# RWKV-5 followed by a squared-ReLU expert: one column of w_in read ahead, diagonal sums of twelve units by VectorE, and a new order table

## The chip, the cores and the metric

The kernel runs on one core of a Trainium2 chip. A core has five engines with a queue each: TensorE (matmuls; PE in the profile, PEld for its weight loads), VectorE (DVE), ScalarE (ACT), GpSimd (POOL) and SyncE (SP, which here only issues DMAs). All DMAs go through 16 DMA engines. On-chip data lies in SBUF, matmul results in eight PSUM banks. The metric is the device time of one execution in microseconds (us), lower is better.

## The reference

```python
def _attn_ref(r, k, v, w, u):            # B, H, S, D = 4, 8, 768, 48
    state = np.zeros((B, H, D, D))
    for t in range(S):
        cur = np.einsum('bhd,bhe->bhde', u[None] * kt, vt)
        y[:, :, t] = np.einsum('bhd,bhde->bhe', rt, state + cur)
        state = w[None, :, :, None] * state + np.einsum('bhd,bhe->bhde', kt, vt)
...
def _moe_ref(x, w_in, w_out):            # 3072 tokens, 384 -> 2048 -> 384
    h = x @ w_in
    r = np.maximum(h, 0.0)
    return (r * r) @ w_out
```

The output y of the recurrence, with the heads side by side, is x. Everything is float32 at the borders.

## The kernel before

The sequence is cut into six chunks of 128 steps. A chunk of one batch is a unit: unit i is batch i % 4 of chunk i // 4, 24 in all. Within a unit the recurrence is matrix work. r is multiplied by rising and k by falling powers of w (`scale`, VectorE, into `rkw`); both are transposed to `rkT`, by TensorE for units 0 to 5 (`turn`, `kb`, evicted by ScalarE) and by a transposing DMA for pairs of units from 6 on (`rkD`, SyncE). `at` makes the 128 x 128 products of k and r for each head, `mask` (VectorE) keeps the strict triangle as `am`, `y` multiplies by v and adds what comes from the running state `stb`. The state is updated by `s` (TensorE), `sadd` and `sdec` (VectorE) and `stb` (ScalarE).

The term with u concerns only the diagonal, where a step meets itself: for each head the sum over d of r k u, times v. Before, it goes like this: `rk` (line 353) multiplies the two halves of `rkT` on VectorE, for a pair at once from unit 6 on; TensorE sums over d with the small matrix `uwb` (u times w, placed head by head), four matmuls to a unit, in a step of its own for units 0 to 3 (line 389) and at the head of `s` for the others (line 410); `dv` (line 420, VectorE) multiplies by v, and `yb` (line 456) adds the result to y. `uwb` holds u times w because the powers in r and k leave one factor of w to be made good there.

The expert follows unit by unit. x is transposed (`xturn` and `xT`, or the DMA `xD`), `m1` multiplies by w_in (line 493), `relu` and `sqA` run on ScalarE, `sqD` is the same square on VectorE (line 510), `m2` multiplies by w_out (line 517), `osb` evicts and `out` stores. w_in comes in four quarters (`I`, line 288) and w_out in four (`O`, line 291), both on GpSimd's queue, where the v loads of units 0 to 5 (`vt`, line 311) stand too. The loads of r and k go over SyncE (lines 281 and 278).

The order of everything on every engine is written out by hand: the table `ORDER` is a list of steps, `name.unit.part@bank`, and a loop at the end of the kernel issues them one after the other. `fill.n` issues n matmuls on a constant tile, whose result nobody reads. What stands ahead of the table in the code (memsets, constants, the first DMAs) comes first on each queue.

Of the kernel before, what the change touches and what calls it, by code (L numbers as in the profile page):

```python
# [21 lines left out]
m1.0.0@7 kbT.1 mask.1.0 turn.2.1@2 relu.0.0 dv.1 rt.5.0 fill.2 y.1@1 rkT.2.1 m1.0.3@4 yb.1 end rt.5.1 s.1@5
scale.3.0 relu.0.3 wend xturn.1@7 rk.2 at.2@26 xT.1 kb.2@0 mask.2.1 sqA.0.0 kt.5.0 d.2@4 turn.3.0@3 vt.3 s.0@7
sadd.1 rkT.3.0 m1.0.2@1 kt.5.1 scale.3.1 kbT.2 O.0 m1.1.0@6 mask.2.0 vb.2 relu.0.2 vt.4 turn.3.1@3 dv.2 m1.1.3@5
rt.6 rkT.3.1 sadd.0 O.1 y.2@1 relu.1.0 kt.6 m1.1.2@0 yb.2 relu.1.3 vt.5 at.3@72 rk.3 relu.1.2 kb.3@4 mask.3.1
xturn.2@6 sqA.1.0 O.2 m1.0.1@5 scale.4.0 xT.2 s.2@0 O.3 sqD.0.3 d.3@2 relu.0.1 m1.1.1@1 vb.3 mask.3.0 turn.4.0@3
kbT.3 m1.2.0@6 scale.4.1 relu.1.1 dv.3 m1.2.1@4 rkT.4.0 sqD.1.3 sqA.0.2 y.3@7 m1.2.2@1 scale.5.0 relu.2.1 sqD.1.1
m1.2.3@2 relu.2.2 sqD.0.1 s.3@5 sqA.1.2 turn.4.1@4 m2.0.0@3 sadd.3 relu.2.3 sadd.2 m2.1.0@1 rkT.4.1 yb.3 relu.2.0
m2.1.1 rk.4 vb.4 scale.5.1 kb.4@7 stb.1 xturn.3@6 at.4@42 kbT.4 m2.0.1 mask.4.1 xT.3 stb.0 s.4@5 mask.4.0 turn.5.0@6
m1.3.0@2 sqD.2.1 rkT.5.0 y.4@0 dv.4 relu.3.0 turn.5.1@6 rt.8 sadd.4 m1.3.3@7 rkT.5.1 yb.4 m2.1.2 sqA.3.0 sqA.2.0  # L30
m2.0.2 kt.8 xturn.4@2 m2.0.3 xT.4 scale.6.0 kb.5@5 osb.0 m2.1.3 scale.7.0 relu.3.3 m1.3.1@2 vtS.6 kbT.5 vb.5
m1.4.0@6 scale.6.1 scale.7.1 at.5@75 relu.4.0 m2.2.0@0 mask.5.0 osb.1 rkD.6 sqA.4.0 m1.4.1@4 sqD.2.3 sqA.2.2 sqD.3.3
m1.4.2@1 relu.3.1 mask.5.1 m2.2.1 stb.3 sdec.4 m1.4.3@6 relu.4.2 rt.10 rk.5 y.5@5 sqA.4.2 scale.8.0 s.5@2 scale.8.1
relu.4.1 m2.2.2 scale.9.0 relu.4.3 vtS.8 m1.3.2@1 sqD.3.1 stb.4 m2.3.0@4 dv.5 relu.3.2 yb.5 m2.2.3 scale.9.1 kt.10
m2.3.1 osb.2 sadd.5 sqA.4.1 m2.4.0@1 sqD.4.3 vb.6 xturn.5@0 sdec.5 at.6@2376 xT.5 rk.6 rkD.8 m2.4.1 stb.2 mask.7.0
stb.5 m1.5.0@0 sqA.3.2 mask.6.0 s.7@7 relu.5.0 mask.7.1 m1.5.3@5 mask.6.1 s.6@2 relu.5.3 m2.4.2 dv.6 out.0 vb.8
y.6@3 dv.7 rt.12 y.7@0 yb.6 m1.5.1@6 yb.7 m2.3.2 sadd.6 relu.5.1 xD.6 scale.10.0 m2.4.3 sqA.5.0 scale.10.1 sqA.5.1
m2.3.3 sadd.7 vtS.10 osb.4 m1.5.2@6 scale.11.1 scale.11.0 m2.5.0@3 relu.5.2 sqD.5.3 kt.12 m2.5.1 sqA.5.2 rk.8
# [24 lines left out]
relu.14.5 sqD.14.3 m1.14.4@7 sqA.14.5 mask.18.0 vtS.22 m2.14.0@3 relu.14.4 dv.18 out.9 m2.15.1 mask.19.1 sqA.14.4
s.19@7 sqA.14.6 rk.20 m2.14.1 sdec.17 y.19@1 dv.19 stb.17 y.18@2 m2.14.2 yb.18 m1.16.0@6 yb.19 sadd.19 xD.18
m1.16.4@2 relu.16.0 sdec.16 m2.14.3 sadd.18 relu.16.4 out.11 m1.16.1@1 osb.14 vb.20 at.20@7256 m1.16.3@4 sqA.16.4
mask.20.1 stb.16 m1.16.2@3 rk.22 relu.16.3 m2.15.2 mask.21.1 relu.16.1 relu.16.2 s.20@4 m2.15.3 dv.20 sqA.16.1
m1.16.5@1 mask.20.0 sqA.16.2 sdec.18 m1.16.7@2 sqA.16.0 mask.21.0 relu.16.5 s.21@7 m1.18.7@6 sdec.19 relu.16.7
s.22@3 sqD.16.3 m1.18.3@1 sqA.16.5 osb.15 m1.18.1@2 vb.22 y.20@4 relu.18.1 m1.16.6@0 yb.20 relu.18.3 y.21@5 dv.21
relu.16.6 m1.18.4@4 sqD.16.7 stb.18 m2.17.0@1 yb.21 relu.18.4 dv.22 m2.16.0@0 xD.20 relu.18.7 sqA.18.1 m2.17.1
sqA.16.6 at.22@3567 out.12 out.15 m1.18.6@4 mask.22.0 out.14 m1.18.2@2 mask.22.1 relu.18.6 m2.17.2 mask.23.0  # L70
relu.18.2 mask.23.1 m2.16.1 stb.19 sqD.18.7 y.22@4 m2.16.2 s.23@2 m1.18.5@7 dv.23 m1.18.0@5 sqD.18.3 yb.22 m2.16.3
relu.18.0 m1.20.0@3 sqA.18.4 relu.18.5 m1.20.3@5 osb.16 m1.20.6@2 relu.20.3 out.16 y.23@6 sqA.18.0 sqD.20.3 m2.17.3
sqA.18.5 yb.23 m1.20.7@4 sqA.18.6 xD.22 sqA.18.2 m1.20.1@7 relu.20.7 m1.20.5@5 relu.20.0 sqD.20.7 m2.18.0@0
relu.20.6 m2.18.1 relu.20.5 sqA.20.6 m2.18.2 sqA.20.0 m2.19.0@5 m2.19.1 m1.20.2@4 m1.20.4@3 relu.20.2 m1.22.6@6
sqA.20.2 m1.22.3@4 relu.20.1 relu.20.4 m2.19.2 osb.17 m2.18.3 sqA.20.5 relu.22.6 m1.22.1@3 relu.22.3 m1.22.0@2
sqA.20.1 sqD.22.3 m2.19.3 relu.22.0 m1.22.7@1 osb.19 sqA.22.0 m2.21.0@2 sqA.20.4 m2.21.1 relu.22.1 m1.22.2@7
sqA.22.6 m1.22.4@6 relu.22.2 m1.22.5@5 relu.22.7 relu.22.4 m2.20.0@3 sqD.22.7 sqA.22.1 m2.21.2 osb.18 sqA.22.2
m2.20.1 relu.22.5 m2.22.0@7 sqA.22.5 m2.22.1 sqA.22.4 m2.20.2 m2.21.3 m2.20.3 osb.21 m2.22.2 out.21 osb.20 out.18
# [5 lines left out]
def kernel(  # L84
# [21 lines left out]
    NH = 6  # L106
# [516 lines left out]
```

## Time and profile before

| | |
|---|---|
| median of 3 runs | 170.97 us (170.62 to 171.13) |
| the profiled execution | 171.94 us |
| its span, first to last instruction | 170.2 us |
| TensorE matmul busy | 163.9 us, 96% |
| ScalarE busy | 129.8 us, 76% |
| VectorE busy | 122.3 us, 72% |
| GpSimd busy | 15.7 us, 9% |
| mean granted TensorE clock | 0.988 |

The profile is of one execution, taken by the hardware. Times in it are counted from the first instruction. Durations of instructions on one engine overlap a little at their ends, so the step from one start to the next is shorter than the duration when an engine runs without a gap. A row of a timeline has the start, the time to the end of the last of the group, the engine, the line and the operation, and in brackets the idle time ahead of it with what ended it.

### The profile page before, as it was taken

The numbers are of one execution on the slowest core, as the hardware profiler recorded it, in microseconds if no ns is written. First come the engines' busy times: TensorE is split into PE (matmuls) and PEld (weight loads), VectorE is DVE, ScalarE is ACT, GpSimd is POOL, SyncE is SP. The second block draws the span as 40 slices with busy tenths as digits, with TensorE's granted clock in tenths as the row PEclk, the third lists the DMA queues.
The fourth block names the chain that finished last, engine by engine and source line by source line (L and its number), as shares of the span: only waits on it lengthen the run. The fifth ranks groups of instructions, "written<-read, shape, count | busy, mean of one in ns | idle before, by whom it ended". The sixth has DMA issues, their size and how long they took to land.

```text
span 170.2 us, 4733 instructions
## 1 busy us (share of the span) xinstructions
PE 163.9 (96%) x1947; PEld 134.1 (79%) x1947; DVE 122.3 (72%) x243; ACT 129.8 (76%) x255; POOL 15.7 (9%) x36
## 2 busy tenths in 40 slices
PE   7959999999999999999999999999999999999993
PEld 7649999778787697886977887787889789688672
DVE  6567999876999989988988888989697662101100
ACT  3735999888796489698499679688699739599921
POOL 7770670000000000000000000000000000000000
PEclk9996999999999999999999999999999999999999
DMA  3999999999999899999999997998990501100044
GB/s 92 172 279 240 272 194 254 213 201 227 185 181 218 153 214 190 181 212 191 236 182 202 174 251 173 188 288 197 180 232 4 179 6 54 42 0 4 0 164 162
DMA packets 91493, 28.86 MB, mean 170 GB/s; under 512 B 82864, under 2 KB 90672, under 8 KB 91472
## 3 DMA queue, kind: packets, MB, share of 16 engines
q1 hardware_dynamic: 88416, 23.99, 67.5%
q0 software_dynamic: 2624, 4.33, 12.9%
q8 instruction: 15, 0.25, 0.6%
q10 hardware_dynamic: 432, 0.25, 0.6%
q14 instruction: 6, 0.05, 0.1%
HBM read 20.50 MB, written 4.72 MB: 148 GB/s over the span
## 4 chain that ended last, share of the span: by engine, by line
PE 87%; DMA 6%; DVE 3%; SPq 2%; issue 1%; DVEq 0%
PE bank L493 36%; PE bank L517 34%; DMA rt<-in_r_dram 4%; PE bank L369 4%; PE bank L441 3%; DMA xT<-yb 2%; PE bank L398 2%; PE bank L447 2%; SPq L281 2%; PE bank L533 2%; PE bank L333 1%; PE bank L410 1%; PE bank L345 1%; PE bank L216 1%; PE bank L477 1%
## 5 line engine op out<-in xcount | busy, mean ns | idle before, releaser
L493 PE MATMUL bank<-xT,w_in_q 128*128 128x256 bf16 (+1 forms) x720 | 72.6, 251 | 0.1
L501 ACT ACTIVATE gr<-bank 128x512 f32<-128x512 f32 x96 | 55.3, 604 | 19.0 <-PE bank L493 15.2
L517 PE MATMUL bank<-w_out_q,g 128*128 128x384 bf16 x368 | 68.6, 326 | 0.0
L493 PEld LDWEIGHTS <-w_in_q 128*128 128x128 bf16 x720 | 63.8, 113 | 3.9 <-DMA xT<-yb 0.3
L517 PEld LDWEIGHTS <-g 128*128 128x128 bf16 x368 | 34.3, 98 | 18.1 <-issue 0.2
L508 ACT ACTIVATE g<-gr 128x512 bf16<-128x512 f32 x68 | 41.2, 636 | 0.2
L377 DVE TENSOR_TENSOR am<-bank,smask 128x512 bf16<-128x512 f32 x48 | 31.3, 684 | 7.4 <-PE bank L369 6.6
L510 DVE TENSOR_TENSOR g<-gr 128x512 bf16<-128x512 f32 x28 | 19.0, 686 | 17.2 <-ACT gr L501 17.2
L524 ACT COPY osb<-bank 128x384 f32<-128x384 f32 x23 | 11.0, 480 | 5.7 <-PE bank L517 5.6
L456 DVE TENSOR_TENSOR yb<-bank,dv 128x384 bf16<-128x384 f32 x24 | 12.9, 553 | 3.2 <-PE bank L447 2.3
L420 DVE TENSOR_TENSOR dv<-vb,bank 128x384 f32<-128x384 bf16 x24 | 13.0, 548 | 2.2 <-PE bank L410 1.4
L432 ACT CAST stb<-st 128x384 bf16<-128x384 f32 x20 | 10.2, 522 | 0.6 <-DVE st L428 0.6
L301 DVE TENSOR_TENSOR rkw<-rt,wpos 128x384 bf16<-128x384 f32 x18 | 9.8, 551 | 0.8 <-DMA rt<-in_r_dram 0.7
L301 DVE TENSOR_TENSOR rkw<-kt,wneg 128x384 bf16<-128x384 f32 x18 | 9.7, 551 | 0.8 <-DMA kt<-in_k_dram 0.8
L337 ACT COPY rkT<-bank 128x512 bf16<-128x512 bf16 x12 | 7.0, 590 | 3.4 <-PE bank L333 3.4
L216 PE MATMUL bank<-warm 128*128 128x128 bf16 x87 | 8.4, 265 | 1.1 <-DVE warm L161 1.1
L441 PE MATMUL bank<-vb,am 128*128 128x48 bf16 x192 | 8.9, 185 | 0.0
L428 DVE TENSOR_TENSOR st<-st,wend 128x384 f32<-128x384 f32 x16 | 8.8, 550 | 0.0
L424 DVE TENSOR_TENSOR st<-bank,st 128x384 f32<-128x384 f32 x16 | 8.7, 549 | 0.0
L441 PEld LDWEIGHTS <-am 128*128 128x128 bf16 x192 | 7.9, 97 | 0.8
L369 PE MATMUL bank<-rkT 64*128 64x128 bf16 x192 | 8.2, 221 | 0.2 <-ACT rkT L337 0.2
L216 PEld LDWEIGHTS <-warm 128*128 128x128 bf16 x87 | 7.0, 121 | 1.2 <-DVE warm L161 1.0
(75 smaller groups left out, 120.8 us busy)
## 6 DMA issues: line engine op xcount, KB each, us to landing
out_dram<-osb SPq DMA_DIRECT2D x23, 192.0 KB, 2.4
rt<-in_r_dram SPq DMA_DIRECT2D x9, 384.0 KB, 5.8
kt<-in_k_dram SPq DMA_DIRECT2D x9, 384.0 KB, 5.2
vt<-in_v_dram SPq DMA_DIRECT2D x9, 384.0 KB, 4.5
w_in_q<-in_moe_w_in_dram POOLq DMA_DIRECT2D x4, 384.0 KB, 8.3
w_out_q<-in_moe_w_out_dram POOLq DMA_DIRECT2D x4, 384.0 KB, 8.8
vt<-in_v_dram POOLq DMA_DIRECT2D x6, 192.0 KB, 7.3
kt<-in_k_dram SPq DMA_DIRECT2D x11, 96.0 KB, 5.2
```

The lines of the kernel that those rows point to most:

```text
L216: nc.tensor.matmul(out=banks[0][:, :128], lhsT=warm, rhs=warm, start=True, stop=True)
L301: nc.vector.tensor_tensor(t["rkw"][:, x, :, :, :D], pair(src), pair(wneg if x else wpos), ALU.mult)
L369: nc.tensor.matmul(out=t["at"][o][:, p, :], lhsT=t["rkT"][sl, 1, p, :], rhs=t["rkT"][sl, 0, p, :], start=True, stop=True,)
L377: nc.vector.tensor_tensor(am, t["at"][o], smask.unsqueeze(1).to_broadcast([C, HP, C]), ALU.mult)
L420: nc.vector.tensor_tensor(t["dv"], t["vb"], t["d"].unsqueeze(2).to_broadcast([C, H, D]), ALU.mult)
L441: nc.tensor.matmul(out=y[:, 2 * p + o, :], lhsT=t[f"am{o}"][:, p, :], rhs=t["vb"][:, 2 * p + o, :], start=(o == 0 and p == 0), stop=c == 0 ...
L456: nc.vector.tensor_tensor(t["yb"], t["y"], t["dv"].rearrange("p h d -> p (h d)"), ALU.add)
L493: nc.tensor.matmul(out=t["h", s][:, a], lhsT=turned, rhs=chunks[c]["xT"][:, b : b + m, n, :], start=(n == 0), stop=(n == NK - 1),)
L501: nc.scalar.activation(t["gr", s], t["h", s], AF.Relu)
L508: nc.scalar.activation(g, x, AF.Square)
L510: nc.vector.tensor_tensor(g, x, x, ALU.mult)
L517: nc.tensor.matmul(out=t["o"], lhsT=chunks[units[i][0]]["g"][:, f, units[i][1], :], rhs=w_out_q[f // 4][:, f % 4, :], start=(f == 0), stop ...
```

## The change

Three things change, and a new table places them.

`ahead` is a tile of 128 x 1 that nobody reads. A DMA on GpSimd's queue fills it with the first column of the first 128 rows of w_in, ahead of the memsets and DMAs for `wu`, which become a step `wu` at the head of the table. The logarithm `lnw` becomes a step too.

For units 12 to 23 the diagonal sum leaves TensorE. `dx` multiplies r and k as they lie in `rkw`, without the transpose, for a pair; `du` multiplies by `uw`, a row of u times w on every partition; `dr` adds up the 48 elements of each head into `dd`. All three are on VectorE. `dv` then takes `dd`. The `rk` products and the four matmuls of each of these units go, and the last chunk's `s` steps with them, which held nothing else. The row `uw` is made once on GpSimd from two broadcast loads, `uB` and `wB`, and lies in the place of `lnat`. `dv` has two buffers for pairs and not four for units. `rk`'s buffers serve `dx`.

Four squares (`sqD.12.3`, `sqD.14.3`, `sqD.16.3`, `sqD.18.3`) become `sqA`. There are 76 fill matmuls, before 87. The parameters `stbP` and `outP` that the diff brings are in no row of the table.

```diff
 ORDER = """
-kt.0.0 kt.0.1 rt.0.0 rt.1.0 I.0 rt.1.1 vt.0 ktA.1.0 lnat.0 fill.26 log@4567 kt.1.1 lnat.1 ids rt.2.0 w.1 upper w.0
...
+wu rt.0.0 kt.0.0 kt.0.1 rt.1.0 lnw rt.1.1 vt.0 ktA.1.0 lnat.0 fill.26 log@4567 kt.1.1 lnat.1 w.0 ids rt.2.0 w.1
...
+    ahead = const.tile([128, 1], F32)
+    nc.gpsimd.dma_start(out=ahead, in_=moe_w_in[:128, :1])
     wu = const.tile([HP, 2, 2, 64], F32)
-    nc.gpsimd.memset(wu[:, 0], 1.0)
-    nc.gpsimd.memset(wu[:, 1], 0.0)
-    nc.gpsimd.dma_start(out=wu[:, 0, :, :D], in_=w.rearrange("(p o) d -> p o d", o=2))
-    nc.gpsimd.dma_start(out=wu[:, 1, :, :D], in_=u.rearrange("(p o) d -> p o d", o=2))
...
-    nc.scalar.activation(lnw, wrow, AF.Ln)
...
+    uw = lnat[:, 0].rearrange("p l e -> p (l e)")
+    rows = {}
...
+    def small():
+        nc.gpsimd.memset(wu[:, 0], 1.0)
+        nc.gpsimd.memset(wu[:, 1], 0.0)
+        for n, src in enumerate((w, u)):
+            nc.gpsimd.dma_start(out=wu[:, n, :, :D], in_=src.rearrange("(p o) d -> p o d", o=2))
+
+    def log_row():
+        nc.scalar.activation(lnw, wrow, AF.Ln)
...
+    def spread_row(name):
+        rows[name] = mpool.tile([128, dm], F32, name="osb")
+        src = dict(uB=u, wB=w)[name].rearrange("h d -> (h d)")
+        nc.gpsimd.dma_start(out=rows[name], in_=src.unsqueeze(0).to_broadcast([128, dm]))
+
+    def uw_row():
+        nc.gpsimd.tensor_tensor(uw, rows["uB"], rows["wB"], ALU.mult)
...
+    def by_rows(i):
+        return i >= NH and f" dx.{i // 2 * 2} " in ORDER.replace("\n", " ")
+
+    def rows_of(i):
+        whole = two("rk", i, work, [128, HP, C], bufs=RKB)
+        return whole.rearrange("p u a c -> p u (a c)")[:, :, :dm]
+
+    def diag_product(i):
+        x = rkw_b[i // 2 % NPAD].rearrange("p u x a o e -> p u x (a o) e")[:, :, :, :, :D]
+        nc.vector.tensor_tensor(rows_of(i).rearrange("p u (h d) -> p u h d", h=H), x[:, :, 0], x[:, :, 1], ALU.mult)
+
+    def diag_weigh(i):
+        whole = of_two("dv", i, work, [C, H, D], F32, bufs=2)
+        nc.vector.tensor_tensor(
+            whole.rearrange("p u h d -> p u (h d)"), rows_of(i), uw.unsqueeze(1).to_broadcast([128, 2, dm]), ALU.mult
+        )
+
+    def diag_add(i):
+        whole = of_two("dd", i, work, [C, H], F32, bufs=3)
+        nc.vector.tensor_reduce(whole, two("dv", i, work, [C, H, D], F32, 2), axis=mybir.AxisListType.X, op=ALU.add)
...
-        if not apart(i):
+        if not apart(i) and not by_rows(i):
             tiles[i]["d"] = d = whole[:, dm : dm + H]
...
-            state_product(i, whole[:, :dm].rearrange("p (a d) -> p a d", a=HP), apart(i))
+            state_product(i, whole[:, :dm].rearrange("p (a d) -> p a d", a=HP), apart(i) or by_rows(i))
...
-        t["dv"] = work.tile([C, H, D], F32, name="dv")
-        nc.vector.tensor_tensor(t["dv"], t["vb"], t["d"].unsqueeze(2).to_broadcast([C, H, D]), ALU.mult)
+        of_two("dv", i, work, [C, H, D], F32, bufs=2)
+        d = t["dd"] if by_rows(i) else t["d"]
+        nc.vector.tensor_tensor(t["dv"], t["vb"], d.unsqueeze(2).to_broadcast([C, H, D]), ALU.mult)
```

The table moves work on every engine. Three places follow, as the built programs have them, with the line numbers of the kernel they belong to.

GpSimd at its start, before (`wu` holds w and u for the transposition into columns, `vt` is unit 0's v, `w_in_q` the first quarter of w_in, `ident` and `identb` the identities):

```order
L164 IOTA iota_i 128x1
L166 MEMSET wu 4x128
L167 MEMSET wu 4x128
L168 DMA wu<-in_w_dram 4x2x48
L169 DMA wu<-in_u_dram 4x2x48
L288 DMA w_in_q_147<-in_moe_w_in_dram 128x3x512
L311 DMA vt<-in_v_dram 128x8x48
masks.py:197 MEMSET ident_100 4x4
```

The same place in the changed kernel:

```order
L165 IOTA iota_i 128x1
L167 DMA ahead<-in_moe_w_in_dram 128x1
L219 MEMSET wu 4x128
L220 MEMSET wu 4x128
L222 DMA wu<-in_w_dram 4x2x48
L222 DMA wu<-in_u_dram 4x2x48
L328 DMA vt<-in_v_dram 128x8x48
masks.py:197 MEMSET ident_98 4x4
masks.py:199 AFFINE_SELECT ident_98<-ident_98 4x4
masks.py:197 MEMSET identb 128x128
masks.py:199 AFFINE_SELECT identb<-identb 128x128
L305 DMA w_in_q_144<-in_moe_w_in_dram 128x3x512
```

The read of `ahead` is first, and the first quarter of w_in has moved behind unit 0's v and both identities.

GpSimd further on, in the changed kernel, from the third quarter of w_in to the end of its work (`osb` names the buffers that `uB` and `wB` fill, `lnat` is where `uw` lies):

```order
L305 DMA w_in_q_146<-in_moe_w_in_dram 128x3x512
L305 DMA w_in_q_145<-in_moe_w_in_dram 128x3x512
L282 DMA osb<-in_u_dram 128x384
L328 DMA vt<-in_v_dram 128x8x48 x2
L308 DMA w_out_q_148<-in_moe_w_out_dram 128x1536
L308 DMA w_out_q_149<-in_moe_w_out_dram 128x1536
L277 COPY wend<-wend_c 64x4x48 x2
L308 DMA w_out_q_150<-in_moe_w_out_dram 128x1536
L308 DMA w_out_q_151<-in_moe_w_out_dram 128x1536
L282 DMA osb<-in_w_dram 128x384
L285 TENSOR_TENSOR lnat<-osb 128x384
L328 DMA vt<-in_v_dram 128x8x48
```

And before, from the last quarter of w_in:

```order
L288 DMA w_in_q_148<-in_moe_w_in_dram 128x3x512
L268 COPY wend<-wend_c 64x4x48 x2
L311 DMA vt<-in_v_dram 128x8x48
L291 DMA w_out_q_151<-in_moe_w_out_dram 128x1536
L311 DMA vt<-in_v_dram 128x8x48
L291 DMA w_out_q_152<-in_moe_w_out_dram 128x1536
L311 DMA vt<-in_v_dram 128x8x48
L291 DMA w_out_q_153<-in_moe_w_out_dram 128x1536
L291 DMA w_out_q_154<-in_moe_w_out_dram 128x1536
```

`wend` (the decay of a whole chunk) has moved from the head of this stretch to the middle of w_out, and unit 5's v from the third place among the loads to the last, behind `uw`.

VectorE at units 12 and 13, before (`rk` is their product of the transposed r and k, `am` the masked products, `st` the state, `dv` the diagonal term from a PSUM bank):

```order
L424 TENSOR_TENSOR st_3_140<-bank_79,st_3_140 128x384
L357 TENSOR_TENSOR rk<-rkT 128x1024
L301 TENSOR_TENSOR rkw_130<-rt,wpos 128x8x48
L301 TENSOR_TENSOR rkw_130<-kt,wneg 128x8x48
L428 TENSOR_TENSOR st_2_139<-st_2_139,wend 128x384
L301 TENSOR_TENSOR rkw_130<-kt,wneg 128x8x48
L510 TENSOR_TENSOR g<-gr 128x2x256
L377 TENSOR_TENSOR am_1678<-bank_77,smask 128x512
```

And in the changed kernel (`rk<-rkw` is `dx`, `dv<-rk,lnat` is `du`, `dd<-dv` is `dr`):

```order
L388 TENSOR_TENSOR rk<-rkw_126 128x2x384
L415 TENSOR_TENSOR am_1496<-bank_280,smask 128x512
L463 TENSOR_TENSOR st_2_136<-bank_282,st_2_136 128x384
L467 TENSOR_TENSOR st_0_134<-st_0_134,wend 128x384
L459 TENSOR_TENSOR dv<-vb,bank_282 128x384
L463 TENSOR_TENSOR st_3_137<-bank_77,st_3_137 128x384
L392 TENSOR_TENSOR dv<-rk,lnat 128x768
L459 TENSOR_TENSOR dv<-vb,bank_77 128x384
L495 TENSOR_TENSOR yb<-bank_281,dv 128x384
L495 TENSOR_TENSOR yb<-bank_279,dv 128x384
L398 TENSOR_REDUCE dd<-dv 128x16
```

One instruction per pair has become three, set among the work of units 10 and 11 before the masks of units 12 and 13.

More of the change, by code (lines that the diff above doesn't have):

```diff
@@ L22 @@
[L22 to L26, printed above, removed]
@@ L77 @@
[L77 to L79 removed]
+wu rt.0.0 kt.0.0 kt.0.1 rt.1.0 lnw rt.1.1 vt.0 ktA.1.0 lnat.0 fill.26 log@4567 kt.1.1 lnat.1 w.0 ids rt.2.0 w.1
+scale.0.0 I.0 fill.7 cols@3 rt.2.1 wk scale.0.1 turn.0.0@1 upper copied kt.2.0 turn.0.1@2 rkT.0.0 vt.1 kt.2.1
@@ L80 @@
+m2.23.0@7 osb.21 out.19 out.20 out.18 m2.22.2 osb.23.0 out.21 m2.22.3 out.23.0 m2.23.1@4 osb.22 out.22 osb.23.1
+out.23.1
 """
```

130 lines of the change are left out of this document (68 added, 62 removed).

## The prediction

> **What bounds the kernel now.** I read the page's busy shares and chain first, then the stages, then single rows of the start.
>
> ```profile
> PE 163.9 (96%) x1947; PEld 134.1 (79%) x1947; DVE 122.3 (72%) x243; ACT 129.8 (76%) x255; POOL 15.7 (9%) x36
> ...
> PE 87%; DMA 6%; DVE 3%; SPq 2%; issue 1%; DVEq 0%
> ```
>
> The chain that ended last is TensorE for 87% of the span. The other 13% must be placed, so the next view cuts the span into stages (busy us and counts per engine, granted clock, DMA share, GB/s).
>
> ```profile
> core 0: us, PE busy (x) PEld busy (x) DVE busy (x) ACT busy (x) POOL busy (x), PEclk, DMA share, GB/s
> 0.00:16.20 16.20, 12.79 (x158) 10.94 (x159) 10.01 (x32) 7.50 (x15) 9.87 (x27) 0.89 0.90 192
> 16.20:60.00 43.80, 43.80 (x665) 36.23 (x662) 40.22 (x78) 36.74 (x77) 5.82 (x9) 1.00 1.02 211
> 60.00:80.00 20.00, 20.00 (x236) 16.55 (x234) 17.87 (x35) 18.18 (x35) 0.00 (x0) 1.00 1.04 195
> 80.00:100.00 20.00, 19.94 (x223) 16.58 (x221) 17.81 (x35) 15.31 (x29) 0.00 (x0) 1.00 1.09 202
> 100.00:120.00 20.00, 20.00 (x234) 15.58 (x232) 18.21 (x35) 15.87 (x30) 0.00 (x0) 1.00 1.05 221
> 120.00:145.00 25.00, 25.00 (x275) 21.44 (x274) 16.08 (x30) 19.94 (x39) 0.00 (x0) 1.00 0.49 106
> 145.00:170.20 25.20, 22.32 (x174) 16.81 (x171) 2.08 (x4) 16.29 (x33) 0.00 (x0) 0.98 0.17 59
> ```
>
> From 16.2 us on TensorE is never idle for longer than a few hundredths. There the time is the sum of TensorE's work, and every matmul that goes is worth its step. Before 16.2 us the kernel waits for data and warms up. VectorE is idle for 2.13, 2.19 and 1.79 us in the three stages between 60 and 120 us (6.1 together) and for 8.9 us between 120 and 145.
>
> The start, from the timelines of TensorE, VectorE, GpSimd and SyncE, with one piece of the chain and two slices of the stage view:
>
> ```profile
> 2.94 0.82 POOL L288 DMA_DIRECT2D w_in_q<-in_moe_w_in_dram  x1
> ...
> 3.67 6.36 DMA rt<-in_r_dram
> ...
> 10.13 0.56 DVE L303 TENSOR_TENSOR rkw<-rt,wfour 128x384 bf16<-128x384 f32 x1 [1.63 <-DMA rt<-in_r_dram]
> ...
> 10.74 0.40 PE L333 MATMUL bank<-identb,rkw 128*128 128x128 bf16 x4 [1.84 <-DVE rkw L303]
> ...
> 11.01 0.75 POOL L288 DMA_DIRECT2D w_in_q<-in_moe_w_in_dram  x1
> ...
> 12.68 0.60 SPq L281 DMA_DIRECT2D kt<-in_k_dram  x1
> ...
> 12.00:13.00 1.00, 0.80 (x13) 0.62 (x11) 0.81 (x2) 0.17 (x1) 0.00 (x0) 0.70 1.11 194
> 13.00:14.00 1.00, 1.00 (x18) 1.00 (x15) 0.63 (x2) 0.95 (x2) 0.00 (x0) 0.50 1.16 215
> ...
> 16.26 0.83 PE L493 MATMUL bank<-xT,w_in_q 128*128 128x128 bf16 x12
> ...
> 23.58 0.83 PE L493 MATMUL bank<-xT,w_in_q 128*128 128x128 bf16 x12
> ```
>
> The second half of unit 1's r (issued at 3.67) lands 6.36 us later, behind the first quarter of w_in (issued at 2.94). VectorE waits for it, TensorE behind VectorE (1.84 us), and the granted clock then falls to 0.70 and 0.50. The first expert matmul starts at 16.26.
>
> **The change, part by part. Diagonal matmuls.** Units 12 to 23 lose four matmuls of `rk` by `uwb` each.
>
> ```profile
> 114.28 0.26 PE L410 MATMUL bank<-uwb,rk 128*128 128x8 bf16 x4
> 114.39 0.33 PE L398 MATMUL bank<-vb,rkw 128*128 128x96 bf16 x4
> ...
> 127.44 0.24 PE L410 MATMUL bank<-uwb,rk 128*128 128x8 bf16 x4
> 127.55 0.83 PE L493 MATMUL bank<-xT,w_in_q 128*128 128x256 bf16 x6
> ```
>
> From the start of four to the start of what follows pass 0.11 us, with a weight load each. Twelve units make 12 x 0.11 = 1.3 us; other places show 0.10, so I take **1.2 us** saved. TensorE is full there, so all of it counts. The 11 fill matmuls that go are waiting time and save nothing.
>
> **VectorE's new work.** Rows of its timeline and of the groups:
>
> ```profile
> 75.15 0.68 DVE L357 TENSOR_TENSOR rk<-rkT 128x1024 bf16<-128x1024 bf16 x1
> 75.75 0.55 DVE L301 TENSOR_TENSOR rkw<-rt,wpos 128x384 bf16<-128x384 f32 x1
> 76.22 0.55 DVE L301 TENSOR_TENSOR rkw<-kt,wneg 128x384 bf16<-128x384 f32 x1
> ...
> L508 ACT ACTIVATE g<-gr 128x512 bf16<-128x512 f32 x68 | 41.2, 636 | 0.2
> L377 DVE TENSOR_TENSOR am<-bank,smask 128x512 bf16<-128x512 f32 x48 | 31.3, 684 | 7.4 <-PE bank L369 6.6
> L510 DVE TENSOR_TENSOR g<-gr 128x512 bf16<-128x512 f32 x28 | 19.0, 686 | 17.2 <-ACT gr L501 17.2
> ```
>
> Packed steps are 0.60 us for 1024 bf16 elements (75.15 to 75.75) and 0.47 for 384 f32 ones, about 0.09 shorter than the durations. 512 f32 elements take 0.684, as long as 1024 bf16, and 384 take 0.55: 0.13 us for 128 f32 elements, half for bf16. A pair's `dx` (768 bf16) is then 0.47 us as a step if it runs like L357, 0.87 if like f32; I take 0.47, since its types are L357's. `du` (768, one operand f32) is 0.87. No row shows a reduction; `dr` reads 768 f32 elements, 0.87 by the same slope, and 1.7 at twice that as upper bound. The old `rk` (0.60) goes. A pair adds 0.47 + 0.87 + 0.87 - 0.60 = 1.6 us, six pairs 9.7. Four squares move to ScalarE: VectorE -2.4 (0.60 each), ScalarE +2.2 at most (0.55 each), which its idle time of 1.8 to 5.1 us in the stages covers. Between 60 and 120 us lie four pairs: 6.4 - 2.4 = 4.0 us against 6.1 idle. It fits, with 2 us to spare; if the cover is gone, `yb`, the transpose of x and the expert matmuls behind it come late, one for one.
>
> **The start.** The first quarter of w_in goes behind the first v and the identities on GpSimd, some 2.3 us later (0.76 `ahead`, 0.96 v, 0.3 memsets, 0.75 identities, less what stood there). Unit 1's loads no longer share the engines with it. One step takes the 1.84 us wait away, and perhaps the slow clock (0.30 + 0.50 in the two slices shown). But the weights and x decide how far TensorE can move:
>
> ```profile
> w_in_q<-in_moe_w_in_dram POOLq DMA_DIRECT2D x1, 384.0 KB, 11.0
> ...
> kt<-in_k_dram SPq DMA_DIRECT2D x1, 96.0 KB, 8.7
> ...
> 1.56 0.76 POOL L168 DMA_DIRECT2D wu<-in_w_dram  x1 [0.31 <-POOL wu L167]
> ```
>
> The last quarter, issued at 11.01, lands 11.0 us later at 22.0 and is first used at 23.58: 1.6 us of room, and the new order has 0.2 us more TensorE work ahead of that use, so 1.4. The DMA issued at 12.68 lands at 21.4. In its slot now stands unit 4's second half of r, whose transposes come some 3 us of TensorE work earlier than before. If it lands no earlier, hardly anything is gained; with the hole at 3 to 7 us filled by x it should land a microsecond sooner. Bounds: +0.76 us of loss (`ahead` is issued before everything else on GpSimd, at L168's price) and 2.6 us of gain (1.84 + 0.80). I take **1.2 us** saved, near the room of 1.4. `ahead` itself is costed at nothing beyond this; what it may save on w_in no row shows.
>
> **A wait that the change adds.** On GpSimd the product `uw` waits until `wB` has landed, and unit 5's v is issued only behind it.
>
> ```profile
> POOL wend L268 <- ACT wend_c L263: 6.9, 1, 6.9
> ...
> w_out_q<-in_moe_w_out_dram POOLq DMA_DIRECT2D x2, 384.0 KB, 10.1
> ...
> vt<-in_v_dram POOLq DMA_DIRECT2D x1, 192.0 KB, 4.8
> ...
> 38.25 0.54 ACT L318 CAST vb<-vt 128x384 bf16<-128x384 f32 x1
> ...
> L268 POOL COPY wend<-wend_c x2: 342/475/608, 18.6 to 19.3; 64x192 f32<-64x192 f32 x2
> ```
>
> Before, the last two w_out quarters are issued near 23.6 and land 10.1 later, at 33.7. The 6.9 us wait ahead of `wend` mostly goes, so GpSimd issues earlier, but the queue is as long and has two rows more; I put `wB` at 33 to 34.5. `uw` takes 0.6 to 1 us (L268's largest as lower end), the v issue 0.9, its landing 4.8 as for an issue into an emptying queue: 39.5 to 41. ScalarE casts it before everything behind it, and unit 5's state product needs it at about 40 (28.1 us of TensorE steps ahead of it and 12 us of start). So 0 to 1.5 us are lost here. With what VectorE may add I take **0.7 us** for all new waits, bounds 0 and 3.5.
>
> The Trainium skill (SBUF — State Buffer, "Who interferes with whom") says that a GpSimd instruction reading SBUF and a VectorE instruction with two SBUF inputs exclude each other. That would speak against `uw`, which runs beside a full VectorE; by it one instruction is held once, at most about 1 us as an estimate from the L268 row, and the sum would be 0.3 to 1 us higher. No run here shows it.
>
> **The sum.** 1.2 + 1.2 - 0.7 = 1.7 us saved. The profiled execution took 171.94 us (span 170.2, 1.74 around it), so 170.2 on that footing; the median of the runs is 170.97, 0.97 lower, so **169.2 us**. A measurement of this kernel tells about 0.3% (0.5 us) from no change.
>
> **The rivals.**
> - *The start gives nothing.* The late first quarter of w_in pushes the last one past 23.6 us, or unit 4's r lands at 21.4 as before. For it: DMA share 1.02 and more up to 120 us. Against it: the quarters behind the first are issued at nearly the old times (GpSimd then stood at 8.6 to 11). Time: 170.97 - 1.2 + 0.7 = 170.5.
> - *VectorE becomes the bound between 60 and 140 us (slower).* If `dx` runs at the f32 rate and `dr` at twice its price, a pair adds 1.6 + 0.4 + 0.8 = 2.8 us; four pairs less the squares make 8.8 against 6.1 idle, of which waits for TensorE (L377's 6.6 us over the kernel) leave about 5 usable. TensorE then loses 3.8 us and more: 170.97 - 2.4 + 3.8 = 172.4. It decides once the lost time passes 2.4 us; with `dr` alone at 1.3 it is 171.
> - *The start gives all.* 2.6 us and no new waits: 170.97 - 1.2 - 2.6 = 167.2.
> - *The GpSimd and VectorE exclusion* by the rule above: 169.9.
>
> **How the numbers follow.** Forecast (168.2 to 170.0) 0.45; start gives nothing 0.18; VectorE bound 0.20; start gives all 0.13; exclusion 0.04. Faster by over 0.3% means below 170.46: 0.45 + 0.13 + 0.04 + half of the second, 0.71. Within 0.3%: the other half, 0.09. Slower: 0.20. The range leaves out the further half of VectorE's case (0.10) and less than half of the lowest (0.05): 167.3 to 171.6.
>
> **What the profile would show.** Right: the diagonal group at 32 matmuls, not 80; first expert matmul at 13.5 to 15; no VectorE wait of 1.6 us for r; `dx` near 0.55 us, `du` and `dr` near 0.95 as durations; VectorE over 93% busy from 60 to 120 us with TensorE still full. Wrong: TensorE waiting for VectorE (`yb`, `am`) or for x's transposes after 60 us; TensorE idle near 40 us at unit 5's state product; the first expert matmul early but gaps for w_in or r until 25 us.

## The result, and the profile after

The changed kernel takes 176.45 us (median of 4 runs, 175.96 to 177.1), the kernel before 171.05 in the same session. The ratio is 1.0312, 95% interval 1.0277 to 1.0348: slower by 5.3 us. I had forecast 169.2 us and given "slower" 0.20; the time lies outside the range. The profiled execution took 177.1 us with a span of 174.1 us, 3.9 us more than the profiled execution before.

The page of the changed kernel: span, busy shares, granted clock by slices, the DMA queue of the loads and transposes, and the chain.

```profile
span 174.1 us, 4647 instructions
...
PE 162.6 (93%) x1888; PEld 132.6 (76%) x1888; DVE 129.2 (74%) x251; ACT 132.5 (76%) x259; POOL 19.3 (11%) x40
...
PEclk9999699999999999999999999999999999999999
...
q1 hardware_dynamic: 88416, 23.99, 72.2%
...
PE 71%; DMA 22%; POOL 4%; issue 1%; DVE 1%; POOLq 0%; DVEq 0%
```

TensorE's share of the chain fell from 87% to 71%, that of the DMAs rose from 6% to 22%. Before, the row of the same DMA queue was

```profile
q1 hardware_dynamic: 88416, 23.99, 67.5%
```

The same number of packets with the same 23.99 MB took 67.5% of the 16 DMA engines' span before (114.9 us of each engine) and 72.2% after (125.7 us). This row led to the cause. (A profiled execution may lie at either end of its kernel's runs: the 19 runs of before beside the first four experiments had spans from 168.2 to 170.8 us, and the profiled one, 170.2 at a mean clock of 0.988, stands near the top.)

Where TensorE loses time, from the stages and from its timeline (the bracket is the idle time ahead of the row and what ended it; the DMA share adds up the times of packets, and passes 1 where packets of one engine overlap):

```profile
core 0: us, PE busy (x) PEld busy (x) DVE busy (x) ACT busy (x) POOL busy (x), PEclk, DMA share, GB/s
0.00:16.20 16.20, 13.00 (x193) 11.20 (x194) 12.67 (x37) 10.44 (x21) 14.57 (x33) 1.00 0.88 194
16.20:60.00 43.80, 41.73 (x600) 34.32 (x597) 36.70 (x70) 34.37 (x69) 4.70 (x8) 0.96 1.10 203
60.00:80.00 20.00, 18.76 (x216) 15.81 (x212) 18.85 (x37) 15.20 (x29) 0.00 (x0) 1.00 1.18 198
80.00:100.00 20.00, 18.88 (x213) 15.78 (x214) 18.61 (x36) 16.45 (x33) 0.00 (x0) 1.00 1.13 198
100.00:120.00 20.00, 19.01 (x199) 14.60 (x197) 18.67 (x34) 17.51 (x34) 0.00 (x0) 1.00 1.02 212
```

```profile
14.29 0.83 PE L532 MATMUL bank<-xT,w_in_q 128*128 128x128 bf16 x12
...
18.32 3.67 PE L532 MATMUL bank<-xT,w_in_q 128*128 128x128 bf16 x36 [1.78 <-DMA w_in_q<-in_moe_w_in_dram]
...
68.66 0.62 PE L407 MATMUL bank<-rkT 64*128 64x128 bf16 x16 [1.04 <-DMA rkT<-rkw]
80.76 0.62 PE L407 MATMUL bank<-rkT 64*128 64x128 bf16 x16 [0.96 <-DMA rkT<-rkw]
92.08 0.62 PE L407 MATMUL bank<-rkT 64*128 64x128 bf16 x16 [0.36 <-DMA rkT<-rkw]
108.10 0.85 PE L532 MATMUL bank<-xT,w_in_q 128*128 128x256 bf16 x6 [0.99 <-DMA xT<-yb]
```

The first expert matmul starts 2 us earlier than before (14.29, was 16.26). Then the second step of the expert waits 1.78 us for its quarter of w_in, and behind the gap the clock is low: 36 matmuls take 3.67 us. The low clock is not what makes the kernel slow: one of its four runs had a mean clock of 1.0 and took 176.01 us all the same. After 60 us, where TensorE was full before, it waits four times for a transposing DMA, 3.35 us together. VectorE is 94% busy there, as forecast, but no row says that TensorE waits for it, and from 60 to 108 us the chain holds no step of VectorE. The four transposes in it are these (start, us, what):

```profile
60.96 7.65 DMA rkT<-rkw
...
72.84 7.87 DMA rkT<-rkw
...
84.18 7.85 DMA rkT<-rkw
...
102.61 5.45 DMA xT<-yb
```

### The profile page after: what moved, and what is told of

The parts are those of the page before. It is cut to its first block, busy times and chain, and to the rows that moved or that the text cites. A ratio compares the mean times of both kernels' runs of the same rounds, so it can differ in the third digit from the quotient of the medians.

```text
span 174.1 us, 4647 instructions
## 1 busy us (share of the span) xinstructions
PE 162.6 (93%) x1888; PEld 132.6 (76%) x1888; DVE 129.2 (74%) x251; ACT 132.5 (76%) x259; POOL 19.3 (11%) x40
## 3 DMA queue, kind: packets, MB, share of 16 engines
q1 hardware_dynamic: 88416, 23.99, 72.2%
## 4 chain that ended last, share of the span: by engine, by line
PE 71%; DMA 22%; POOL 4%; issue 1%; DVE 1%; POOLq 0%; DVEq 0%
PE bank L556 30%; PE bank L532 29%; DMA rkT<-rkw 13%; DMA w_in_q<-in_moe_w_in_dram 5%; PE bank L407 3%; DMA xT<-yb 3%; PE bank L480 2%; PE bank L436 2%; PE bank L572 2%; POOL vt L328 1%; PE bank L486 1%; PE bank L350 1%; POOL wu L222 1%; POOL w_in_q L305 0%; POOL ahead L167 0%
## 5 line engine op out<-in xcount | busy, mean ns | idle before, releaser
L532 PEld LDWEIGHTS <-w_in_q 128*128 128x128 bf16 x720 | 64.8, 115 | 6.8 <-DMA w_in_q<-in_moe_w_in_dram 2.0
L547 ACT ACTIVATE g<-gr 128x512 bf16<-128x512 f32 x72 | 43.7, 637 | 0.3
L549 DVE TENSOR_TENSOR g<-gr 128x512 bf16<-128x512 f32 x24 | 16.3, 686 | 17.2 <-ACT gr L540 17.1
L459 DVE TENSOR_TENSOR dv<-vb,bank 128x384 f32<-128x384 bf16 x12 | 6.5, 549 | 5.1 <-PE bank L427 4.1
L407 PEld LDWEIGHTS <-rkT 64*128 64x128 bf16 x192 | 5.4, 94 | 5.4 <-DMA rkT<-rkw 3.4
L333 ACT CAST vb<-vt 128x768 bf16<-128x768 f32 x9 | 7.5, 834 | 0.7 <-DMA vt<-in_v_dram 0.7
```

The lines of the kernel that those rows point to most:

```text
L407: nc.tensor.matmul(out=t["at"][o][:, p, :], lhsT=t["rkT"][sl, 1, p, :], rhs=t["rkT"][sl, 0, p, :], start=True, stop=True,)
L532: nc.tensor.matmul(out=t["h", s][:, a], lhsT=turned, rhs=chunks[c]["xT"][:, b : b + m, n, :], start=(n == 0), stop=(n == NK - 1),)
L547: nc.scalar.activation(g, x, AF.Square)
L549: nc.vector.tensor_tensor(g, x, x, ALU.mult)
```

## The experiments

Three theories stood at the start. A: the transfers are a second bound beside TensorE, and the new order puts their stream behind. B: VectorE, nearly full, makes the scaled tiles and so the transposes late. C: the read-ahead itself, first on GpSimd's queue, spoils the start. A fourth, D, came out of the first results. Ratios are to the kernel before, with 95% intervals, its runs taken on the same chip in the same session (medians 170.6 to 171.2 us).

### The read-ahead alone, and everything but it

```diff
+    ahead = const.tile([128, 1], F32)
+    nc.gpsimd.dma_start(out=ahead, in_=moe_w_in[:128, :1])
```

The first experiment adds these two lines to the kernel before, the second takes them out of the changed kernel.

> The kernel before with nothing but the read-ahead of one column of w_in put first on GpSimd. Theory A (the transfers are a second bound beside TensorE from about 18 us on, and the new order puts their stream about 3 us behind) expects next to nothing of this small transfer beyond its issue: the first quarter of w_in is issued 0.7 us later, the time is 171.0 to 171.8. Theory C (the read-ahead itself, first on GpSimd's queue, spoils the start) expects 172.5 or more, with a wait for w_in's last quarter. If the read-ahead makes w_in land sooner, the time falls below 170.5.

Measured: 172.81 us, ratio 1.0111 (1.0077 to 1.0146).

> The changed kernel without the read-ahead, its table as it is. Theory A: the quarters of w_in are issued 0.7 us earlier, the wait for the third one shrinks from 1.8 to about 1.1 us, and the waits for transposed tiles after 60 us stay: 175.5 to 176.5. Theory C: most of the 5 us goes, 172 to 173. If w_in's landing was helped by the read-ahead, the first expert matmuls wait longer and the time is above 177.

Measured: 172.58 us, ratio 1.0089 (1.0055 to 1.0123). So a DMA of 512 bytes costs 1.1% in the one kernel and 2.2% (1.0312 to 1.0089) in the other. Theory A had it at nothing. But C does not fit the start: with the read-ahead alone the first expert matmul starts at 14.5 us and no wait for w_in is longer than 0.4 us. What differs between the pages is the queue of the loads, read-ahead alone first, then without it:

```profile
q1 hardware_dynamic: 88416, 23.99, 73.9%
```

```profile
q1 hardware_dynamic: 88416, 23.99, 67.5%
```

The packets take longer, and not at the start alone, and the tile `ahead` moves every tile behind it: in the built programs it takes 32 bytes of each partition, and r, k, v, rkT, xT, yb, w_in, w_out and the output buffers start at 32 and not at 0 modulo 64 bytes. (rkw, from which the transposes of r and k read, goes the other way, from 32 to 0.) That this place makes the packets slow, and they the kernel, is theory D.

### The place without the transfer, the transfer without the place

```diff
+    pad = const.tile([128, 8], F32, name="pad")
     wu = const.tile([HP, 2, 2, 64], F32)
```

> The kernel before with an unused tile of 32 bytes where the read-ahead's tile would stand, and no transfer. Theory D: the packets of the loads take 73 to 74% as with the read-ahead and the time is 172.3 to 173.3 (before 171.0, read-ahead alone 172.8). Theory C: nothing changes, 170.7 to 171.3 and 67.5%.

Measured: 172.28 us, ratio 1.0069 (1.0034 to 1.0103). The queue of the loads on its page:

```profile
q1 hardware_dynamic: 88416, 23.99, 73.4%
```

Nothing is transferred, no instruction is added, and the kernel is slower with the packets at 73.4%. The engines' own work is no slower on the moved tiles: the masks on VectorE take 683 ns each (684 before), ScalarE's relu 601 (604), the m2 matmuls 326 in both. So the place costs, by way of the DMAs: 0.7% in the kernel before. The 0.4% between this and the read-ahead (1.0069 to 1.0111) cannot be told from zero, and C is not needed.

```diff
-    ahead = const.tile([128, 1], F32)
-    nc.gpsimd.dma_start(out=ahead, in_=moe_w_in[:128, :1])
+    ahead = const.tile([128, 16], F32)
+    nc.gpsimd.dma_start(out=ahead[:, :1], in_=moe_w_in[:128, :1])
```

> The changed kernel with the read-ahead, but its tile made 16 columns wide (64 bytes to a partition, of which the DMA fills the same one column). New theory D: it is not the transfer but the place that costs. The tile takes 32 bytes of SBUF, and every tile behind it, r, k, v, rkT, xT, w_in, w_out and the output buffers, then starts at 32 and no longer at 0 modulo 64 bytes; the same 88416 packets of the loads took 72.2% of the DMA engines' span and not 67.5%. D expects the packets back at 67 to 68% and 172.6 to 173.3 us (the kernel without the read-ahead had 172.6, the issue may cost 0.7). If the transfer or its place in the queue costs (theory C), 175.5 to 176.5 and 72%.

Measured: 172.92 us (4 runs), ratio 1.0139 (1.0061 to 1.0217). The time is what D expected, the queue's row is not all the way back:

```profile
q1 hardware_dynamic: 88416, 23.99, 69.6%
```

With 64 columns in the place of 16, the tile is 256 bytes wide:

> The changed kernel with the read-ahead's tile made 256 bytes wide, the same one column filled, so that all tiles behind it stand modulo 256 bytes as without it. With the tile of 64 bytes the packets took 69.6% of a span of 172.7 us, 120 us of each DMA engine's time, between 115 (without) and 126 (32 bytes). Theory D with a step at 256 bytes: 115 us of packet time and 172.3 to 173. With a step at 64 bytes alone: as with 64 bytes, 120 us and 172.9.

Measured: 172.67 us, ratio 1.0097 (1.0061 to 1.0133). Its page, and the rows of TensorE's timeline that answer to those above:

```profile
q1 hardware_dynamic: 88416, 23.99, 66.8%
```

```profile
14.34 0.83 PE L532 MATMUL bank<-xT,w_in_q 128*128 128x128 bf16 x12
...
17.58 2.20 PE L532 MATMUL bank<-xT,w_in_q 128*128 128x128 bf16 x36 [0.36 <-DMA w_in_q<-in_moe_w_in_dram]
...
66.51 0.62 PE L407 MATMUL bank<-rkT 64*128 64x128 bf16 x16 [0.47 <-DMA rkT<-rkw]
...
104.08 0.85 PE L532 MATMUL bank<-xT,w_in_q 128*128 128x256 bf16 x6 [0.56 <-ACT osb L563]
```

This is the changed kernel, instruction for instruction, with its tiles moved back to where the kernel without the read-ahead has them, modulo 256 bytes. 1.0312 becomes 1.0097: the place costs 2.15%, 3.7 of the 5.3 us. Between 60 and 110 us the rows show where: of 3.35 us of waits 1.03 are left (1.18 with the tile of 64 bytes, 0.87 without the read-ahead). At the start they are no proof. The waits for w_in shrink from 1.78 to 0.88 us (0.36 and, at 23.90, 0.52) and the slow clock goes, but the profiled execution of the 64-byte tile, 175.28 us where its three other runs took 172.8 to 173.0, has them both:

```profile
19.11 3.35 PE L532 MATMUL bank<-xT,w_in_q 128*128 128x128 bf16 x36 [2.24 <-DMA w_in_q<-in_moe_w_in_dram]
```

So this gap comes and goes from run to run without a shift of 32 bytes. Between 1.0097 with the transfer and 1.0089 without it lies nothing that can be told from zero: the transfer itself costs nothing that these runs can measure.

The trace's packet records say which packets it is. The table gives, from the profiled executions, the start of the tiles r, k, v, rkT, yb, w_in and w_out modulo 64 and 256 bytes (xT and the output buffers agree modulo 64), the time of one DMA engine on the 55296 packets of 192 bytes (the loads of r, k and v from unit 6 on, 48 floats a head), on the 25344 packets of 256 bytes (the transposes), and on the whole queue (its share times the span).

| kernel | start mod 64 / 256 | 192 B, us | 256 B, us | queue, us |
|---|---|---|---|---|
| before | 0 / 0 | 53.6 | 38.9 | 114.9 |
| changed, no read-ahead | 0 / 0 | 54.3 | 36.5 | 114.7 |
| changed, tile of 256 bytes | 0 / 0 | 53.8 | 36.8 | 114.1 |
| changed, tile of 64 bytes | 0 / 64 | 54.5 | 42.6 | 120.2 |
| before + 32 bytes | 32 / 32 | 60.6 | 42.1 | 126.0 |
| before + read-ahead | 32 / 32 | 59.9 | 42.1 | 125.7 |
| changed | 32 / 32 | 60.3 | 41.4 | 125.7 |

The small packets of the loads take 11% longer off a 64-byte start in the changed kernel (54.3 to 60.3) and 13% in the one before (53.6 to 60.6), and are indifferent to 64 or 256. All traces of this case agree: 53.6 to 55.9 us where the tiles start at 0 modulo 64, 59.9 to 62.4 where they start at 32. The Trainium skill (DMA: Bandwidth & Descriptors, "How a descriptor splits into AXI transactions") says that a transaction starts at a 256-byte boundary, the bytes ahead of the wanted ones being fetched for nothing, in beats of 32 bytes. An estimate by it, each packet taken as one descriptor: packets of 192 bytes one behind the other take 9 beats on average from a start at 0 or 64, and 10 from 32, 11% more. The trace agrees in size, on the written side, which is the one that moved here and of which the page's rule does not speak. The transposes' packets scatter more from run to run; in the last two transposes of x, when nothing else moves, they take 0.86 us of each engine in before and 0.98 to 0.99 at 32 / 32 and 0 / 64. So these packets seem not to be indifferent to 64 or 256; but early_half below, at 0 / 0, has 0.89 and 1.29.

### VectorE's diagonal in the table of before

```diff
-... rk.12 ... mask.13.0 ... mask.12.1 ... mask.12.0 ... mask.13.1 ... dv.12 ...
+... dx.12 ... mask.13.0 ... mask.12.1 du.12 ... mask.12.0 ... mask.13.1 ... dr.12 dv.12 ...
```

The other pairs go the same way, and uB, wB and uw stand behind the last quarter of w_out.

> The table of before, with the diagonal sums of units 12 to 23 on VectorE (dx in the place of rk, du between the masks, dr ahead of dv), uB, wB and uw behind the last quarter of w_out, no read-ahead. Theory B (VectorE, 94% busy between 60 and 120 us, makes the scaled tiles and with them the transposes late): slower by 3 us or more, 174 and above, with TensorE waiting after 60 us. Theory A (the table's order of transfers does it): TensorE's work falls by 1.2 us, but the transfers get 0.39 MB more (about 2 us at 200 GB/s) and TensorE catches up with them: 170.5 to 172, with small waits for transposed r and k after 60 us.

Measured: 173.69 us, ratio 1.0128 (1.0068 to 1.0188). The stages from 80 to 120 us:

```profile
80.00:100.00 20.00, 18.40 (x196) 14.70 (x194) 19.63 (x37) 14.46 (x28) 0.00 (x0) 1.00 1.12 205
100.00:120.00 20.00, 19.04 (x205) 14.71 (x203) 19.93 (x36) 15.34 (x30) 0.00 (x0) 1.00 1.10 220
```

and the rows of TensorE's timeline there that have waits:

```profile
80.95 0.36 PE L476 MATMUL bank<-vb,am 128*128 128x48 bf16 x8 [0.27 <-DVE am L411]
...
84.35 0.36 PE L476 MATMUL bank<-vb,am 128*128 128x48 bf16 x8 [0.91 <-DVE yb L491]
...
92.15 0.36 PE L476 MATMUL bank<-vb,am 128*128 128x48 bf16 x8 [0.40 <-DVE am L411]
...
119.68 0.27 PE L476 MATMUL bank<-vb,am 128*128 128x48 bf16 x4 [0.96 <-DVE am L411]
```

Here VectorE is full (19.93 of 20 us) and TensorE does wait for it, at the masks and at yb, 2.6 us in 40. That is my rival of a full VectorE, with dx, du and dr at the prices I had taken (below); it needs no dearer reduction, only an order without room. The changed table moves four squares to ScalarE and spreads the three steps, and no such wait occurs in it: B is not what costs there.

### The stores on another queue

```diff
-... out.0 ... out.15 ...
+... outP.0 ... outP.15 ...
```

> The changed kernel with the stores of units 0 to 15 on GpSimd's queue, which is idle after 42 us, and not on SyncE's. The bytes are the same. If SyncE's queue, in which every issue stands behind the last, is what delays the transposes, the four waits of TensorE between 68 and 108 us (4.0 us together) shrink to under 1.5 us and the time falls to 172.5 to 174.5. If the DMA engines themselves are full (theory A in its strict form), the transposes land as late as before and the time stays within 1 us of 176.4. Theory B too expects 176.4.

Measured: 178.48 us, ratio 1.0424 (1.0354 to 1.0495), slower than the changed kernel itself. Taking the stores off SyncE's queue does not free TensorE: r and k of pair 10 land at 69.7 us (68.6 in the changed kernel) and x of pair 14 at 108.8 (108.1); the waits for pairs 12 and 14 go, one of 0.87 us for pair 16 comes, and between 60 and 110 us TensorE waits 3.76 us for transposes (3.35). So it is not the stores ahead of them in SyncE's queue that make TensorE wait.

### Half of each table

Both take the table of one kernel up to about 55 us and the order of the other behind it, without the read-ahead, with the tiles at 0 modulo 64.

> The first 339 steps of the changed table (without uB, wB and uw), then the order of before, with the diagonal on TensorE throughout; no read-ahead. If the changed start is worth nothing or less, as the two profiles of the start say (delay of TensorE 12.95 us at 22 us against 12.9 at 23.8), 170.7 to 172; if it is the part that loses, 172.3 to 173; if it gains what I forecast, 169.8.

Measured: 171.88 us, ratio 1.0053 (1.0015 to 1.0091). The changed start loses 0.9 us (0.3 to 1.6), where I forecast 1.2 us of gain.

> The first 340 steps of the table of before (to about 55 us), then the changed table's order, with the diagonal of units 12 to 23 on VectorE and uB, wB and uw at the seam; no read-ahead. TensorE's work is 1.2 us less than before. If the changed start is what the changed kernel without the read-ahead loses (1.6 us against before), this runs in 169.5 to 170.5. If VectorE or the transfers take the gain back after 60 us (theories A and B), 171 to 172.5, with waits for the transposed x or r and k, or for the masks.

Measured: 173.6 us, ratio 1.0155 (1.0063 to 1.0247). This trial spoilt itself at the seam: uB and wB hold two output buffers until `uw` is made, ScalarE waits for a free one, and TensorE for ScalarE, as its timeline says:

```profile
60.87 0.24 PE L444 MATMUL bank<-uwb,rk 128*128 128x8 bf16 x4 [2.12 <-ACT osb L559]
```

> As late_half, but uB, wB and uw follow the last quarter of w_out (about 24 us) and no longer hold two output buffers at the seam, for which TensorE waited 2.1 us at 60.9 us there. If the diagonal on VectorE pays with this order of the later half, 169.5 to 170.5 (TensorE's work is 1.2 us less than before). If VectorE or the transfers take it back, 171 to 172, with waits of TensorE after 60 us of 1 us and more.

Measured: 170.99 us, ratio 1.0011 (0.9970 to 1.0052). The wait is gone and TensorE is full, as the stages show:

```profile
60.00:80.00 20.00, 20.00 (x223) 16.30 (x221) 20.00 (x39) 17.31 (x34) 0.00 (x0) 1.00 1.04 208
80.00:100.00 20.00, 20.00 (x231) 16.80 (x228) 19.62 (x37) 17.80 (x35) 0.00 (x0) 1.00 1.03 198
100.00:120.00 20.00, 19.72 (x206) 15.26 (x204) 18.45 (x35) 15.91 (x31) 0.00 (x0) 1.00 1.08 213
```

TensorE has 1.2 us less work, and the time is that of before, at best 0.5 us lower. VectorE runs at 97%, and the DMA share is 1.03 to 1.08. Two kernels relieve the one or the other and give up a part of the result for it: the first leaves out du and dr, so that units 12 to 23 lack the term with u, the second stores only 96 of 384 columns of units 0 to 15.

```diff
-... du.12 ... dr.12 ...
+...
-        d = t["dd"] if by_rows(i) else t["d"]
+        d = none[:, :H] if by_rows(i) else t["d"]
```

> late_half_2 with du and dr left out (dv multiplies by a constant, so the output lacks the term with u in units 12 to 23): VectorE has 11 us less work between 60 and 140 us, the transfers are the same. If VectorE is what eats the 1.2 us, 169.3 to 170; if the transfers do, 170.5 to 171.2 as late_half_2.

Measured: 170.89 us, ratio 0.9976 (0.9940 to 1.0013).

```diff
-        queue.dma_start(out=out[b * S + c * C : b * S + (c + 1) * C, :], in_=tiles[i]["osb"])
+        n = 96 if i < 16 else dm
+        queue.dma_start(out=out[b * S + c * C : b * S + (c + 1) * C, :n], in_=tiles[i]["osb"][:, :n])
```

> late_half_2 with the stores of units 0 to 15 cut to their first 96 of 384 columns (the output is not complete): 2.4 MB less, some 11 us of the stream at 210 GB/s, VectorE's work as it was. If the transfers are the second bound, 169.3 to 170.2; if VectorE is, as late_half_2, 170.5 to 171.2.

Measured: 170.64 us, ratio 0.9968 (0.9929 to 1.0008). Each is 0.6 to 0.7 us below late_half_2 (1.0011 to 0.9976 and to 0.9968), but all the intervals overlap: neither relief is told from none, nor from the other, and neither brings the 169.3 to 170 us that its theory expected. Where the diagonal's 1.2 us go stays open.

### GpSimd's small product earlier

```diff
-... vt.1 ... wr zeros ... vt.2 ... I.3 ... uwb ...
+... vt.1 ... wr ... zeros uwb vt.2 ... I.3 ...
```

> early_half with GpSimd's product for uwb two DMA issues earlier, ahead of unit 2's v and w_in's last quarter. In early_half TensorE's first diagonal sum waits 1.2 us for it at 10.2 us. If that wait is what the changed start loses, 170.8 to 171.2 (early_half 171.9); if the loads set the start, 171.6 to 172, with the wait moved to the transposes of unit 2 or to w_in.

Measured: 171.52 us, ratio 1.0017 (0.9989 to 1.0045), against 1.0053 of early_half. The direction is the expected one, but my premise was not: in the trace of early_half the 1.2 us ahead of the first diagonal sum are fill matmuls and no wait for `uwb` (in the changed kernel itself that wait is 0.95 us). With overlapping intervals this shows little. The two profiles differ elsewhere: in early_half a load of r takes 10.5 us to land, VectorE waits for it, and TensorE behind VectorE, which uwb_early doesn't show:

```profile
29.57 0.36 PE L476 MATMUL bank<-vb,am 128*128 128x48 bf16 x8 [1.24 <-DVE dv L455]
```

That is one execution of each; which loads of the changed start cost the 0.9 us is not settled. What is left of the 1.0097 behind the start is not located either.

### The place of rkw

```diff
+    pad0 = const.tile([128, 24], F32, name="pad0")
     rkw_b = [const.tile([128, 2, 2, HP, 2, 64], BF16, name=f"rkw{n}") for n in range(NPAD)]
...
+    pad1 = const.tile([128, 40], F32, name="pad1")
     smask = const.tile([128, 128], F32)
```

> The kernel before with two unused pieces of SBUF (96 bytes ahead of the four rkw buffers and 160 behind), so that rkw, from which the transposing DMAs read, starts at 0 modulo 256 bytes and no longer at 160, all else unmoved modulo 256. If the place of what a DMA reads costs as that of what it writes does (theory D in its wide form), the packets of the loads and transposes fall from 67.5% to 64 to 66% and the time by 0.3 to 1 us: 170.0 to 170.7. If only the written side counts, 67.5% and 171.

Measured: 170.78 us, ratio 0.9996 (0.9956 to 1.0035); the queue's share fell to 66.4%. The tile from which the transposes read, at 160 modulo 256 in before, gains nothing that can be measured by standing at 0.

> late_half_2 with rkw at 0 modulo 256 bytes as well. If both give what they can, 169 to 170; if the place of rkw is worth nothing, as late_half_2.

Measured: 170.56 us, ratio 0.9991 (0.9962 to 1.0020). It is the fastest version with the diagonal on VectorE that computes the whole result, and no faster than before. The row of its queue:

```profile
q1 hardware_dynamic: 88416, 23.99, 71.5%
```

That is nearly the share of the changed kernel, with all tiles in place: its transposes' packets took 41.6 us of an engine, for reasons that I have not found, its 192-byte packets 55.9. So the column of 256 bytes above can scatter by 5 us, and a high share of the queue alone does not make a kernel slow.

## Why the prediction was wrong, point by point

- **What bounds the kernel.** That TensorE is never idle from 16.2 us on was read rightly. That "every matmul that goes is worth its step" does not follow, and failed: in late_half_2, with the work gone and TensorE waiting 0.3 us in all between 60 and 120 us, the time stayed. The DMA share of 1.02 to 1.09 and VectorE at 90% stood in the same rows; that they take the saving back was not shown.
- **Diagonal matmuls, 1.2 us.** The work went as forecast: the group has 32 matmuls in the place of 80, and its steps from start to start add up to 0.8 us, 2.1 before. The time did not fall with it.
- **VectorE's new work.** dx, du and dr measured 0.551, 0.950 and 0.944 us, against 0.55, 0.95 and 0.95 as I had read them off other shapes. In the changed order no wait came of it, and with another order it did. The groups of the changed kernel:

```profile
L392 DVE TENSOR_TENSOR dv<-rk,lnat 128x768 f32<-128x768 bf16 x6 | 5.7, 950 | 0.0
L398 DVE TENSOR_REDUCE dd<-dv 128x16 f32<-128x768 f32 x6 | 5.7, 944 | 0.0
L388 DVE TENSOR_TENSOR rk<-rkw 128x768 bf16<-128x768 bf16 x6 | 3.3, 551 | 0.0
```

- **The start, 1.2 us of gain, bounds 0.76 of loss and 2.6 of gain.** The early first expert matmul came (14.29). The gain did not: early_half measured 0.9 us of loss, 0.3 to 1.6, near the bound of 0.76. I took the room from the last quarter of w_in, but the quarter that is used second is the tight one: its use came at 18.3 us and it landed at 18.27. It was issued at 9.66 us, behind `ahead` and unit 2's v, and took 8.6 us; before, it was issued at 8.58 and there at 15.6. And the slow clock that I meant to save is absent from most executions: 15 of the 19 other runs had a mean clock of 0.998 and more.
- **`ahead`, "costed at nothing beyond this", its issue.** This is the step that failed most: 3.7 of the 5.3 us. I priced the instruction and not the tile, which moves all tiles behind it by 32 bytes. The range had no room for this, since a loss all over the span was in none of its terms. With the 1.2 us of the diagonal that were not gained and the start that lost 0.9 in the place of gaining 1.2, it adds up to 7.0 of the 7.3 us between forecast and result.
- **The added wait, 0.7 us.** GpSimd did wait for wB, 10.4 us long, and nobody waited for GpSimd: unit 5's state product came without a gap. The 3.35 us of waits after 60 us fit into my bounds of 0 to 3.5 by size alone; the mechanism was another one.
- **The rivals.** "The start gives nothing" was right about the start and is 6 us off in the time. The full VectorE did not occur in this table. (In that rival, "with `dr` alone at 1.3 it is 171" does not come out of its own sum, which gives 169.3; 171 belongs to `dr` at 1.7. It bears on none of the chances.) The exclusion of GpSimd and VectorE, which the Trainium skill (SBUF — State Buffer, "Who interferes with whom") states, changes nothing here: `uw` runs once, and nobody waits for it. The wait ahead of it, from the view of waits of the changed kernel:

```profile
POOL lnat L285 <- DMA osb<-in_w_dram: 10.4, 1, 10.4
```

## What to carry to other kernels

A new tile changes the addresses of all tiles behind it, so a small tile belongs at the end of its pool, or is padded so that the tiles that DMAs touch keep their start modulo 64 bytes. Compare the packet time of the same packets, size by size, between two profiles: for the 192-byte loads it tells the two places apart in every trace here, which no single wait does, while the sum over the queue scatters. Work taken off an engine that is never idle need not shorten the time: 1.2 us less on TensorE brought nothing here that could be measured, and the reason stayed open.

## What the runs showed of the hardware

Tiles that start at 32 and not at 0 modulo 64 bytes in SBUF make loads of 192-byte pieces 11 to 13% slower in the DMA engines (54.3 to 60.3 and 53.6 to 60.6 us of each engine); the shift costs the kernel before 0.7% (1.0069) and the changed kernel 2.15% (1.0312 to 1.0097). The last x transpose, alone on the engines, lands 2.5 us after its issue in before and 2.7 to 2.8 us after it with yb at 32 or 64 modulo 256 bytes; early_half, with yb at 0, has 2.8 too, so this is no more than a tendency. Sixteen stores moved from SyncE's queue to GpSimd's, with the same bytes, made the changed kernel 1.1% slower (1.0312 to 1.0424, by intervals that just part). A VectorE reduction of 128 x 768 float32 to 128 x 16 took 0.944 us.
